# Retention and two gated layers on one core: the causal mask formed on the chip instead of loaded, with fewer warming products and other due times

## The chip, the core and the metric

One core of a Trainium2 chip runs the whole program in one launch. The metric is device time in microseconds (us), the median of three runs; lower is better. Before the change it is 601.28 us (600.91 to 601.75). The engines are named as the profile names them: PE (TensorE, products) with its weight loads PEld, DVE (VectorE), ACT (ScalarE), POOL (GpSimd) and SP (SyncE, which only issues transfers here); SPq, ACTq and POOLq are their transfer queues.

## The reference, cut to what matters

Three steps follow one another on 1536 tokens (2 batches of 768) of width 512, which is 8 heads of 64. The first is a retention layer: a state per head that decays by `gamma[h]` at each step.

```python
gamma = 1.0 - 2.0 ** (-5.0 - np.arange(H))
for t in range(S):
    state = gamma[None, :, None, None] * state + np.einsum('bhd,bhe->bhde', k[:, :, t], v[:, :, t])
    y[:, :, t] = scale * np.einsum('bhd,bhde->bhe', q[:, :, t], state)      # scale = 1/8
x = (x @ w_a) * (x @ w_b) @ w_out                                           # 512 -> 1536 -> 512
xn = x / sqrt(mean(x * x) + 1e-6) * rms_g
out = silu(xn @ w_gate) * (xn @ w_val) @ w_out2                             # 512 -> 1536 -> 512
```

## The kernel before

**Retention in chunks.** The tokens are cut into 12 chunks of 128 (`NCH`, two batches interleaved). For chunk n the kernel forms scores k·q of all heads by eight products of 64 rows (`scores`, banks `sc{n}_0` and `sc{n}_1`), multiplies them on DVE by a mask (`p{n}`), and multiplies the values by that (`values`, `ya{n}`). The mask is, for row s and column t of a chunk, scale·gamma^(t−s) where t is at least s, and 0 elsewhere; it is 128 x 1024 numbers, the same for all chunks. What came before the chunk enters by the running state `st` (`state`, from `vd{n}`, the values decayed by DVE or POOL), copied to `sd`, and by decayed queries `qd` (`past`). One more table, `dq_sb`, is formed on the chip already: `decays` multiplies two small matrices loaded as `tables` and copies the result.

**The two gated layers.** They are blocked by 128 hidden columns and 512 tokens; most blocks use a seven-product scheme in place of eight (names P1 to P7, banks `b`, `d`, `x_P`), the first and last blocks of a layer are plain (`c`, `y`). Weights come as 64-bit words (`raw`), are turned into floats by ACT and DVE (`low`, `top`, `middle`, `joined`), and are split into a high and a low part (`uh`, `ul`), so that each product is done in three passes.

**The order of the work.** Nothing is issued as it is written. Each call goes to `Plan.record` as an operation with a cost; at the end `Plan.order` gives every operation a due time, working back from PE's own order (`dues`), adds the number that the table `SHIFTS` holds for that operation's index, and lists the operations of each engine by readiness and due time (`list`). Adding or removing one operation renumbers all later ones. Each engine then runs its list strictly in order. For the retention part the order of recording is the string `HEAD`: `lq0` loads the queries and keys of chunk 0, `lk0` its keys and values in the other layout, `lw` one weight block, `m` is `masks`, `warm13` is thirteen products of a zero tile (`keep_warm`), `S0` the scores of chunk 0, `d` is `decays`, `L1` both loads of chunk 1, `x` steps the weight conversion.

**The loads at the start.** SP issues the mask (512 KB), then `q0`, `raw0_0`, `q1`, `k0`, `k1` of 512 KB each; ACT issues `dg_sb` (decay factors for values, and others), POOL issues `tables`. PE begins with the warming products, which wait for nothing but a memset of DVE.

Of the kernel before, what the change touches and what calls it, by code (L numbers as in the profile page):

```python
# [10 lines left out]
F32 = mybir.dt.float32  # L11
# [10 lines left out]
B, H, S, D = 2, 8, 768, 64  # L22
P = 128
# [3 lines left out]
C = 128  # L27
NCH = NT // C
CPB = S // C
NP = H // 2  # L30
KD = DM // P
NF = DFF // P
TB = 512
# [6 lines left out]
KH = KD // 2 * P  # L40
# [4 lines left out]
TURN = {(64, P): 200, (64, 64): 110, (P, P): 222, (P, 64): 147}  # L45
TABLE = 1283
SHIFTS = {
# [20 lines left out]
}  # L68
ROUNDS = 2
SLOW = 3414  # L70
# [12 lines left out]
LINE = 128  # L83
# [1 line left out]


FIRST = (0, 0), (0, 1), (1, 0), (1, 1)
HEAD = "lq0 lw m lk0 warm13 S0 d L1 lq3 lq2 lk2 x c0 x x lw lk3 x W0 P0 V0 F0 x w1 S1 Q2 L4 x T0 lw lw P1 V1 F1 T1 x x Ha0 S2 P2 V2 F2 Q3 w2 c0 S3 x T2 W3 P3 x x V3 F3 x S4 x T3 L5 L6 D2 Q4 W4 L7 c1 Ua0 x Q5 W5 T4 x Hb0 Ub0 x D3 G0 S5 P4 V4 R0 F4 x L8 Q6 W6 x S6 T5 P5 V5 F5 c1 x L9 Q7 w7 x T6 S7 P6 V6 F6 x L10 D4 Q8 W8 P7 T7 V7 F7 S8 x x L11 q9 W9 x t0 t1 c1 x x Ua1 Ub1 G1 x x S9 P8 R1 x D5 T8 q10 V8 F8 x t1 c1 Ua2 x x Ub2 x G2 x R2 S10 P9 V9 F9 x q11 t1 T9 x Ua3 x x Ub3 G3 S11 x R3 T10 P10 P11 V10 F10 x x t1 V11 F11"
UP = {"P1": (1, 0), "P2": (5, 1), "P6": (4, 2), "P7": (3, 3), "P5": (2, 4), "P3": (7, 5), "P4": (6, 6)}


# [407 lines left out]


@with_exitstack
def retention_glu_swiglu(ctx: ExitStack, tc: tile.TileContext, qk, kv, tb, mask, dg, eye, w1, w2, rg, partial, out):
    nc = tc.nc
    plan = Plan(nc, tc, ctx)

# [27 lines left out]
    vec, act, gps = Engine("vec", 70, 1.04), Engine("act", 100, 0.83), Engine("gps", 120, 2.2)  # L533

    def dma(engine, out, a, regions=(), **k):
        n = 4
        for size in (out if isinstance(out, View) else a).shape:
            n *= size
        kind = "load" if isinstance(out, View) else "acc" if k else "store"
        plan.record(engine, "dma_start", out, (a,), k, 700 if engine == "gps" else 400, n / RATE[kind], kind, regions)  # L540

    def mm(out, *a, **k):
        n = 1
        for size in out.shape[1:]:
            n *= size
        work["pe"] += 0.443 * n if n >= HB else 111
        full = out.shape[0] == P and a[0].shape[0] == P
        each = 0.443 * n if n > HB else 123.6 if n == HB else 111 if full else 111 * (n + 8) / 136 if out.shape[0] == P or a[0].shape[0] == P else 54
        if n == TB and a[0].tile.dtype == F32:
            each = 0.97 * n  # L550
        if n < HB and full and a[0].tile.dtype == F32:
            each = 232
        op = plan.record("pe", "matmul", out, a, k, each, each + 163)
        op.shape = a[0].shape[0], out.shape[0]
# [11 lines left out]
    one = Pool(plan, "one", 1)  # L566
# [822 lines left out]
    if True:  # L1389

        xf = {}
        if True:
# [3 lines left out]

            dq_sb = ac.tile([P, NP, C], F32, name="dq_sb")
            mask_sb = ac.tile([P, 2, NP, C], F32, name="mask_sb")
            dg_sb = ac.tile([P, 3 * LINE // 4], F32, name="dg_sb")
            tables = one.tile([P, 8, KH], F32, tag="uh1", name="tables").rearrange("p k n -> p (k n)")[:2, :P + TB]  # L1400
            dk_sb = dg_sb[:, :CPB * H].rearrange("p (c h) -> p c h", h=H)
            gq_sb = dg_sb[:, CPB * H:CPB * (H + NP)].rearrange("p (c n) -> p c n", n=NP)
            st = bank("S", "st").rearrange("p (b n d) -> p b n d", b=B, n=NP)
            qk_t, kv_t = {}, {}
# [157 lines left out]
            vec.memset(warm, 0.0)  # L1562
            vec.memset(ones32, 1.0)
            act.activation(both[:, n + KD:n + KD + 2], ones32, AF.Sqrt)
            dma("act", dg_sb[:, :CPB * (H + NP)], dg)
            dma("gps", tables, tb)

            def masks(_):
                dma("sp", mask_sb.rearrange("p r n c -> p (r n c)"), mask)

            def decays(_):
                b = bank("A", "decays")
                plan.cut()
                mm(b, tables[:, :P], tables[:, P:], start=True, stop=True)
                plan.follow(plan.group, firsts[0])
                plan.cut()
                act.copy(dq_sb, b.rearrange("p (n c) -> p n c", n=NP))
# [100 lines left out]
def _consts(np):  # L1678
    g = 1.0 - 2.0 ** (-5.0 - np.arange(H, dtype=np.float64))
    t = np.arange(C, dtype=np.float64)  # L1680
    scale = 1.0 / np.sqrt(D)
    up = scale * g[:, None] ** (C + t - S // 2)
    tb = np.concatenate([np.repeat(np.eye(2), D, axis=1), up.reshape(NP, 2, C).transpose(1, 0, 2).reshape(2, NP * C)], axis=1)
    apart = t[None, :] - t[:, None]
    mask = np.where(apart >= 0, scale * g[:, None, None] ** np.maximum(apart, 0), 0)
    mask = mask.reshape(NP, 2, C, C).transpose(2, 1, 0, 3).reshape(C, 2 * NP * C)
    c = np.arange(CPB)[:, None] * C
    dk = g ** (S // 2 - (c + t)[:, :, None]).transpose(1, 0, 2)
    gq = np.repeat((g ** (c - C)).reshape(CPB, NP, 2, 1), D, axis=3).reshape(CPB, NP, P).transpose(2, 0, 1)
    dg = np.concatenate([dk.reshape(P, CPB * H), gq.reshape(P, CPB * NP)], axis=1)  # L1690
    return {n: np.ascontiguousarray(a, dtype=np.float32) for n, a in (("tb", tb), ("mask", mask), ("dg", dg), ("eye", np.eye(P)))}

# [40 lines left out]
```

## Time and profile before

| | us |
|---|---|
| median of 3 runs (lowest, highest) | 601.28 (600.91, 601.75) |
| the profiled execution | 601.72 |
| its span, first to last instruction | 599.9 |
| PE busy (share of the span) | 593.8 (99%) |
| DVE busy | 526.2 (88%) |
| ACT busy | 427.0 (71%) |
| POOL busy | 118.1 (20%) |

The profile is one execution. Busy time of PE is modelled from starts, so a busy PE need not be a PE at its full pace. The profiled execution took 1.8 us more than its span, and it lies near the slowest of the three timed runs. The chain of work that ended last is PE for 98% of the span.

### The profile page before, as it was taken

How to read it: one execution, taken by the hardware profiler on the slowest of the kernel's cores; microseconds unless marked ns; L12 is line 12 of the kernel's file. 1: busy time of each engine (PE TensorE's matmuls, PEld its weight loads, DVE VectorE, ACT ScalarE, POOL GpSimd, SP SyncE). 2: the span in 40 equal slices, each digit the busy share in tenths (PEclk: the TensorE clock that was granted, in tenths of full speed). 3: DMA queues.
4: the chain of work that ended last, by engine and by line, in shares of the span. 5: the costliest groups of instructions: out<-in, count | busy, mean ns of one | idle time of the engine just before them, and what ended most of it. 6: DMA issues, size and time to landing. Idle time of an engine off the chain costs nothing.

```text
span 599.9 us, 9471 instructions
## 1 busy us (share of the span) xinstructions
PE 593.8 (99%) x3342; PEld 496.0 (83%) x3342; DVE 526.2 (88%) x1012; ACT 427.0 (71%) x822; POOL 118.1 (20%) x135
## 2 busy tenths in 40 slices
PE   9999999999999999999999999999999999999997
PEld 8988888888888888888887888888888888888886
DVE  4898995898999999996799999799999999799874
ACT  5666874668787877867555986768988887786730
POOL 2420000014233323233100000003222232322310
PEclk9999999999999999999999999999999999999999
DMA  8894333148889979799930234317988998985886
GB/s 347 324 348 128 110 109 131 61 105 158 178 153 228 184 140 193 142 168 180 284 136 0 86 127 146 135 70 137 178 154 149 174 184 157 187 157 127 153 198 224
DMA packets 40351, 98.24 MB, mean 164 GB/s; under 512 B 4590, under 2 KB 4974, under 8 KB 40304
## 3 DMA queue, kind: packets, MB, share of 16 engines
q0 software_dynamic: 17312, 31.47, 35.7%
q1 hardware_dynamic: 22704, 66.07, 32.8%
q8 instruction: 26, 0.43, 0.3%
q14 instruction: 21, 0.17, 0.1%
q10 hardware_dynamic: 288, 0.10, 0.1%
HBM read 56.73 MB, written 40.89 MB: 163 GB/s over the span
## 4 chain that ended last, share of the span: by engine, by line
PE 98%; DVE 1%; ACT 0%; issue 0%
PE b L498 32%; PE y L498 18%; PE d L498 16%; PE x_P L498 13%; PE c L498 11%; PE ya L498 3%; PE sc L498 2%; PE w L498 1%; PE st L498 1%; PE ms L498 0%; PE rb L498 0%; DVE acc L498 0%; DVE sq L498 0%; DVE g L498 0%; PE decays L498 0%
## 5 line engine op out<-in xcount | busy, mean ns | idle before, releaser
L498 POOL DMA_DIRECT2D out<-z x60 | 52.2, 894 | 233.2 <-ACT z L498 166.7
L498 POOL DMA_DIRECT2D partial<-z x60 | 52.5, 916 | 202.1 <-ACT z L498 166.3
L498 PE MATMUL y<-h,o 128*128 128x512 f32 (+2 forms) x294 | 70.8, 389 | 0.7 <-DVE h L498 0.7
L498 ACT COPY z<-x_P 128x512 f32<-128x512 f32 x88 | 51.3, 588 | 19.5 <-PE x_P L498 18.4
L498 PEld LDWEIGHTS y<-h,o 128*128 128x128 f32 x294 | 53.6, 188 | 11.9 <-DVE h L498 1.2
L498 DVE TENSOR_TENSOR g<-g,d 128x256 f32<-128x256 f32 x134 | 55.2, 414 | 9.3 <-ACT g L498 6.8
L498 PE MATMUL b<-xh,uh 128*128 128x512 f32 x160 | 63.1, 394 | 0.0
L498 PE MATMUL b<-xh,ul 128*128 128x512 f32 x160 | 62.6, 392 | 0.0
L498 PE MATMUL b<-xl,uh 128*128 128x512 f32 x160 | 62.6, 391 | 0.0
L498 PE MATMUL d<-x,uh 128*128 128x512 f32 (+1 forms) x176 | 59.1, 375 | 0.4 <-DVE g L498 0.4
L498 DVE TENSOR_TENSOR ul<-wt,uh 128x512 fp32r<-128x512 f32 x82 | 54.6, 684 | 2.3 <-ACT uh L498 2.0
L498 ACT CAST v<-raw 128x512 f16<-128x512 bf16 x72 | 55.6, 785 | 0.6
L498 ACT CAST uh<-wt 128x512 fp32r<-128x512 f32 x82 | 49.5, 622 | 5.7 <-DVE wt L498 3.8
L498 ACT ACTIVATE v<-raw 128x512 int32<-128x512 uint32 x72 | 47.9, 680 | 7.8 <-DMA raw<-in_w 7.8
L498 PE MATMUL x_P<-r,l 128*128 128x512 f32 x192 | 52.5, 391 | 0.0
L498 ACT COPY z<-y 128x512 f32<-128x512 f32 x56 | 32.7, 588 | 21.6 <-PE y L498 20.1
L498 PE MATMUL y<-h,l 128*128 128x512 f32 x192 | 47.6, 392 | 0.0
L498 PE MATMUL b<-th,uh 128*128 128x512 f32 x120 | 47.2, 393 | 0.0
L498 PE MATMUL b<-th,ul 128*128 128x512 f32 x120 | 46.9, 391 | 0.0
L498 PE MATMUL b<-tl,uh 128*128 128x512 f32 x120 | 46.8, 390 | 0.0
L498 PE MATMUL d<-x,ul 128*128 128x256 f32 x160 | 44.7, 280 | 0.0
L498 PE MATMUL d<-t,uh 128*128 128x512 f32 (+1 forms) x132 | 44.3, 375 | 0.0
(157 smaller groups left out, 1432.3 us busy)
## 6 DMA issues: line engine op xcount, KB each, us to landing
raw<-in_w SPq DMA_DIRECT2D x72, 512.0 KB, 4.8
partial<-z POOLq DMA_DIRECT2D x60, 256.0 KB, 5.5
out<-z POOLq DMA_DIRECT2D x60, 256.0 KB, 5.4
q<-in_qk SPq DMA_DIRECT2D x12, 512.0 KB, 6.4
k<-in_kv SPq DMA_DIRECT2D x10, 512.0 KB, 7.1
partial<-z SPq DMA_DIRECT2D x12, 256.0 KB, 2.4
acc<-partial SPq DMA_DIRECT2D x6, 512.0 KB, 7.5
out<-z SPq DMA_DIRECT2D x12, 256.0 KB, 2.2
```

Source lines behind the costliest of these rows:

```text
L498: getattr(self.engines[op.engine], method)(real(out), *map(real, args), **{k: real(a) for k, a in kwargs.items()})
```

## The change

The mask's transfer is gone. `tables` grows from 2 x 640 numbers to 8 x 1792 (57,344 bytes for 5,120): gamma^−s per head, the two rows used before, and scale·gamma^t laid out so that an eight-row product of the first with one half of the last gives scale·gamma^(t−s) for four heads at once. Two such products (`mask0`, `mask1`, 128 x 512 each) go to PE ahead of the first scores, and DVE multiplies each by a triangle of ones, `tri`, which travels as 128 more columns of `dg_sb` (114,688 bytes for 36,864). Both transfers are now issued by ACT, `tables` first; POOL issues none at the start. The warming products are 8 instead of 13. The planner's cost for a 512-column product of this kind is 2.05 ns a column instead of 0.97, and `SHIFTS` holds other numbers for other indices.

```diff
-HEAD = "lq0 lw m lk0 warm13 S0 d L1 ...
+HEAD = "lq0 lw lk0 warm8 m S0 d L1 ...
@@ SHIFTS (one row of the table)
-    7: -7450, 8: 9900, 17: 14150, 19: 23600, 22: 17750, 39: 16550, 40: 26600, ...
+    18: -6200, 20: 14750, 22: 21950, 25: 15950, 29: 9950, 42: 14050, 43: 21250, ...
@@ mm
-            each = 0.97 * n
+            each = 2.05 * n
@@
-            dg_sb = ac.tile([P, 3 * LINE // 4], F32, name="dg_sb")
-            tables = one.tile([P, 8, KH], F32, tag="uh1", name="tables").rearrange("p k n -> p (k n)")[:2, :P + TB]
+            dg_sb = ac.tile([P, 3 * LINE // 4 + C], F32, name="dg_sb")
+            tables = one.tile([P, 8, KH], F32, tag="uh1", name="tables").rearrange("p k n -> p (k n)")[:H, :tb.shape[1]]
+            tri = dg_sb[:, 3 * LINE // 4:]
@@
-            dma("act", dg_sb[:, :CPB * (H + NP)], dg)
-            dma("gps", tables, tb)
+            dma("act", tables, tb)
+            dma("act", dg_sb, dg)
             def masks(_):
-                dma("sp", mask_sb.rearrange("p r n c -> p (r n c)"), mask)
+                for r in range(2):
+                    b = bank("Y", f"mask{r}")
+                    plan.cut()
+                    mm(b, tables[:, :P], tables[:, 2 * P + r * TB:2 * P + (r + 1) * TB], start=True, stop=True)
+                    plan.cut()
+                    mult(mask_sb[:, r], b.rearrange("p (n c) -> p n c", n=NP), tri[:, None, :].to_broadcast([P, NP, C]))
@@ decays
-                mm(b, tables[:, :P], tables[:, P:], start=True, stop=True)
+                mm(b, tables[:2, P:2 * P], tables[:2, 2 * P + 2 * TB:], start=True, stop=True)
@@ _consts
+    tb[:, :P] = g[:, None] ** -t
+    for h in range(H):
+        at = 2 * P + (h % 2 * NP + h // 2) * C
+        tb[h, at:at + C] = scale * g[h] ** t
+    tri = t[None, :] >= t[:, None]
```

On SP the mask's issue, the first of its queue, is gone, and `q1` stands ahead of `raw0_0`: `q0`, `q1`, `raw0_0`, `k0`, `k1`.

PE at the start of the program, before (the number behind a name is the chunk, `w` the warming bank; the last number tells tiles apart):

```order
L498 MATMUL w_88<-warm_78 128x128 [waits DVE_49]
L498 MATMUL w_88<-warm_78 128x128 x12
L498 MATMUL sc0_0_115<-q0_102 128x128 [waits DMAHW2_49]
...
L498 MATMUL decays_129<-tables_82 128x512 [waits DMASW0_49]
L498 MATMUL sc1_0_137<-q1_107 128x128 [waits DMAHW4_49]
...
L498 MATMUL ya0_0_157<-p0_131,k0_109 64x128 [waits DMAHW5_49,DVE_49]
...
L498 MATMUL st_174<-vd0_167,k0_109 64x64 [waits DVE_49]
```

The same stretch of PE after the change:

```order
L496 MATMUL w_86<-warm_78 128x128 [waits DVE_49]
L496 MATMUL w_86<-warm_78 128x128 x7
L496 MATMUL mask0_106<-tables_80 128x512 [waits DMAHW0_49]
L496 MATMUL mask1_108<-tables_80 128x512
L496 MATMUL sc0_0_112<-q0_82 128x128 [waits DMAHW1_49]
...
L496 MATMUL decays_129<-tables_80 128x512
L496 MATMUL sc1_0_137<-q1_97 128x128 [waits DMAHW2_49,DVE_49]
...
L496 MATMUL st_156<-vd0_147,k0_102 64x64 [waits DMAHW5_49,DVE_49]
```

Five warming products went and two mask products came, which wait for the table on ACT's queue; the state's update of chunk 0 moved ahead of `ya0`; and the scores of chunk 1 now also wait for DVE, since the mask products took two banks of their ring.

DVE at the start, before (`u0_0` is the first weight block, `vd0` the decayed values of chunk 0):

```order
L498 TENSOR_SCALAR u0_0_125<-raw0_0_105 128x512 [waits DMAHW3_49]
L498 TENSOR_TENSOR p0_131<-sc0_0_115,mask_sb_84 128x512 [waits DMAHW1_49,PE_49]
L498 TENSOR_TENSOR p0_131<-sc0_1_117,mask_sb_84 128x512 [waits PE_49]
L498 ISA u0_0_125<-u0_0_125,v0_0_127 128x1024 [waits DVE_49,Activation_49]
L498 TENSOR_TENSOR p1_153<-sc1_0_137,mask_sb_84 128x512 [waits PE_49]
L498 TENSOR_TENSOR vd0_167<-k0_109,dg_sb_80 128x512 [waits DMAHW5_49,DMAHW0_49]
```

The same stretch of DVE after the change:

```order
L496 TENSOR_TENSOR mask_sb_110<-mask0_106,dg_sb_95 128x512 [waits DMAHW3_49,PE_49]
L496 TENSOR_TENSOR mask_sb_110<-mask1_108,dg_sb_95 128x512 [waits PE_49]
L496 TENSOR_SCALAR u0_0_125<-raw0_0_100 128x512 [waits DMAHW4_49]
L496 TENSOR_TENSOR p0_131<-sc0_0_112,mask_sb_110 128x512 [waits DVE_49,PE_49]
L496 TENSOR_TENSOR p0_131<-sc0_1_114,mask_sb_110 128x512 [waits DVE_49,PE_49]
L496 TENSOR_TENSOR vd0_147<-k0_102,dg_sb_95 128x512 [waits DMAHW5_49]
```

Two multiplications stand ahead of everything else on DVE, and `vd0` moved ahead of the second half of the weight conversion (`ISA`) and of `p1`.

PE where the first output products `y` of layer one begin, before (each `y` is six products, of which the first three are shown):

```order
L498 MATMUL y0_1121<-h0_0_0_475,o0_858 128x512 x3
...
L498 MATMUL b1_0_1136<-xh0_0_170,uh2_1129 128x512
...
L498 MATMUL y3_1149<-h0_0_0_475,o0_858 128x512 x3
...
L498 MATMUL y8_1163<-h0_0_2_1134,o0_858 128x512 x3
...
L498 MATMUL d1_6_1181<-x0_2_784,uh2_1129 128x512
```

The same place of PE after the change:

```order
L496 MATMUL y0_1118<-h0_0_0_471,o0_846 128x512 x3
...
L496 MATMUL y1_1132<-h0_0_0_471,o0_846 128x512 x3
...
L496 MATMUL y3_1146<-h0_0_0_471,o0_846 128x512 x3
...
L496 MATMUL y4_1160<-h0_0_1_751,o0_846 128x512 x3
...
L496 MATMUL y6_1174<-h0_0_1_751,o0_846 128x512 x3
```

Nine of the twelve `y` (0, 1, 3, 4 and 6 to 10) now follow one another before the first `d1_6` and `b1_0`; before, they were spread between those.

## Rows read from the trace of the kernel before

**Rows 1.** The page, part 1: busy us of PE, its weight loads, and others.

```profile
PE 593.8 (99%) x3342; PEld 496.0 (83%) x3342; DVE 526.2 (88%) x1012; ACT 427.0 (71%) x822; POOL 118.1 (20%) x135
```

**Rows 2.** Waits of PE: engine, tile, whom it waited for, us, times, longest.

```profile
PE w L498 <- DVE small L498: 1.1, 1, 1.1
PE y L498 <- DVE h L498: 0.7, 1, 0.7
PE d L498 <- DVE g L498: 0.4, 1, 0.4
PE st L498 <- DVE vd L498: 0.3, 1, 0.3
PE rb L498 <- DVE scale L498: 0.2, 1, 0.2
```

**Rows 3.** Stretches: busy PE, PEld, DVE, ACT, POOL; granted clock, DMA share, GB/s.

```profile
0.00:5.00 5.00, 3.94 (x18) 3.94 (x19) 0.17 (x2) 1.49 (x2) 0.88 (x5) 1.00 0.61 210
5.00:8.00 3.00, 3.00 (x26) 2.78 (x24) 0.43 (x1) 0.78 (x2) 0.00 (x0) 1.00 1.03 421
8.00:12.00 4.00, 3.65 (x46) 2.41 (x46) 3.50 (x6) 3.34 (x9) 0.85 (x1) 1.00 1.03 417
```

**Rows 4.** Timeline, first 12 us, PE: start, us, tile, count, [idle before].

```profile
1.06 5.92 PE L498 MATMUL w<-warm 128*128 128x128 f32 x26 [1.06 <-DVE small L498]
6.90 1.31 PE L498 MATMUL sc<-q 64*128 64x128 f32 x16
8.14 1.12 PE L498 MATMUL decays<-tables 2*128 2x512 f32 x2
9.19 1.16 PE L498 MATMUL sc<-q 64*128 64x128 f32 x16
10.28 1.09 PE L498 MATMUL ya<-p,k 128*64 128x128 f32 x16
11.73 0.69 PE L498 MATMUL st<-vd,k 128*64 128x64 f32 x16 [0.35 <-DVE vd L498]
```

**Rows 5.** Tile w: ns of one, least/median/most.

```profile
L498 PEld LDWEIGHTS w<-warm x26: 288/333/333, 1.1 to 6.3; 128*128 128x128 f32 x26
L498 PE MATMUL w<-warm x26: 421/421/582, 1.1 to 6.6; 128*128 128x128 f32 x26
```

**Rows 6.** The page, part 5: groups, busy us and mean ns of one.

```profile
L498 ACT COPY z<-y 128x512 f32<-128x512 f32 x56 | 32.7, 588 | 21.6 <-PE y L498 20.1
L498 PEld LDWEIGHTS y<-h,o 128*128 128x128 f32 x294 | 53.6, 188 | 11.9 <-DVE h L498 1.2
```

**Rows 7.** Timeline, first 12 us, SPq, ACTq and DVE.

```profile
0.74 0.38 SPq L498 DMA_DIRECT2D mask_sb<-in_mask  x1
0.74 0.41 ACTq L498 DMA_DIRECT2D dg_sb<-in_dg  x1
7.19 0.43 DVE L498 TENSOR_SCALAR u<-raw 128x512 int32<-128x512 int32 x1 [6.18 <-DMA raw<-in_w]
8.24 1.29 DVE L498 TENSOR_TENSOR p<-sc,mask_sb 128x512 f32<-128x512 f32 x2 [0.63 <-PE sc L498]
10.99 0.68 DVE L498 TENSOR_TENSOR vd<-k,dg_sb 128x512 f32<-128x512 f32 x1
```

**Rows 8.** Transfers: issuer, count, KB each, median us from issue to landing.

```profile
mask_sb<-in_mask SPq DMA_DIRECT2D x1, 512.0 KB, 3.9
dg_sb<-in_dg ACTq DMA_DIRECT2D x1, 36.0 KB, 4.0
tables<-in_tb POOLq DMA_DIRECT2D x1, 5.0 KB, 4.8
```

**Rows 9.** Waits of PE's weight loads.

```profile
PEld ya L498 <- issue: 1.6, 7, 0.4
PEld sc L498 <- DMA q<-in_qk: 0.8, 1, 0.8
```

More of the change, by code (lines that the diff above doesn't have):

```diff
@@ L87 @@
 FIRST = (0, 0), (0, 1), (1, 0), (1, 1)
-HEAD = "lq0 lw m lk0 warm13 S0 d L1 lq3 lq2 lk2 x c0 x x lw lk3 x W0 P0 V0 F0 x w1 S1 Q2 L4 x T0 lw lw P1 V1 F1 T1 x x Ha0 S2 P2 V2 F2 Q3 w2 c0 S3 x T2 W3 P3 x x V3 F3 x S4 x T3 L5 L6 D2 Q4 W4 L7 c1 Ua0 x Q5 W5 T4 x Hb0 Ub0 x D3 G0 S5 P4 V4 R0 F4 x L8 Q6 W6 x S6 T5 P5 V5 F5 c1 x L9 Q7 w7 x T6 S7 P6 V6 F6 x L10 D4 Q8 W8 P7 T7 V7 F7 S8 x x L11 q9 W9 x t0 t1 c1 x x Ua1 Ub1 G1 x x S9 P8 R1 x D5 T8 q10 V8 F8 x t1 c1 Ua2 x x Ub2 x G2 x R2 S10 P9 V9 F9 x q11 t1 T9 x Ua3 x x Ub3 G3 S11 x R3 T10 P10 P11 V10 F10 x x t1 V11 F11"
+HEAD = "lq0 lw lk0 warm8 m S0 d L1 lq3 lq2 lk2 x c0 x x lw lk3 x W0 P0 V0 F0 x w1 S1 Q2 L4 x T0 lw lw P1 V1 F1 T1 x x Ha0 S2 P2 V2 F2 Q3 w2 c0 S3 x T2 W3 P3 x x V3 F3 x S4 x T3 L5 L6 D2 Q4 W4 L7 c1 Ua0 x Q5 W5 T4 x Hb0 Ub0 x D3 G0 S5 P4 V4 R0 F4 x L8 Q6 W6 x S6 T5 P5 V5 F5 c1 x L9 Q7 w7 x T6 S7 P6 V6 F6 x L10 D4 Q8 W8 P7 T7 V7 F7 S8 x x L11 q9 W9 x t0 t1 c1 x x Ua1 Ub1 G1 x x S9 P8 R1 x D5 T8 q10 V8 F8 x t1 c1 Ua2 x x Ub2 x G2 x R2 S10 P9 V9 F9 x q11 t1 T9 x Ua3 x x Ub3 G3 S11 x R3 T10 P10 P11 V10 F10 x x t1 V11 F11"
 UP = {"P1": (1, 0), "P2": (5, 1), "P6": (4, 2), "P7": (3, 3), "P5": (2, 4), "P3": (7, 5), "P4": (6, 6)}
@@ L501, in retention_glu_swiglu @@
 @with_exitstack
-def retention_glu_swiglu(ctx: ExitStack, tc: tile.TileContext, qk, kv, tb, mask, dg, eye, w1, w2, rg, partial, out):
+def retention_glu_swiglu(ctx: ExitStack, tc: tile.TileContext, qk, kv, tb, dg, eye, w1, w2, rg, partial, out):
     nc = tc.nc
@@ L1682, in _consts @@
     up = scale * g[:, None] ** (C + t - S // 2)
[L1683 to L1686, printed above, removed]
+    tb = np.zeros((H, 2 * P + 3 * TB))
+    tb[:, :P] = g[:, None] ** -t
+    tb[:2, P:2 * P] = np.repeat(np.eye(2), D, axis=1)
+    for h in range(H):
+        at = 2 * P + (h % 2 * NP + h // 2) * C
+        tb[h, at:at + C] = scale * g[h] ** t
+    tb[:2, 2 * P + 2 * TB:] = up.reshape(NP, 2, C).transpose(1, 0, 2).reshape(2, NP * C)
+    tri = t[None, :] >= t[:, None]
     c = np.arange(CPB)[:, None] * C
@@ L1689, in _consts @@
     gq = np.repeat((g ** (c - C)).reshape(CPB, NP, 2, 1), D, axis=3).reshape(CPB, NP, P).transpose(2, 0, 1)
-    dg = np.concatenate([dk.reshape(P, CPB * H), gq.reshape(P, CPB * NP)], axis=1)
-    return {n: np.ascontiguousarray(a, dtype=np.float32) for n, a in (("tb", tb), ("mask", mask), ("dg", dg), ("eye", np.eye(P)))}
+    dg = np.concatenate([dk.reshape(P, CPB * H), gq.reshape(P, CPB * NP), np.zeros((P, 3 * LINE // 4 - CPB * (H + NP))), tri], axis=1)
+    return {n: np.ascontiguousarray(a, dtype=np.float32) for n, a in (("tb", tb), ("dg", dg), ("eye", np.eye(P)))}
 def _layout(np, i):
```

38 rows, old and new, of the table SHIFTS are left out of this document.

## The prediction

> **What bounds the kernel now.** I read the page's busy times first: PE is busy for 593.8 of 599.9 us [rows 1], so a change pays only if it takes work from PE or one of the few times that PE waits. The list of PE's waits comes next, and it is short [rows 2]: 1.1 us at the very start, 0.3 for the decayed values of chunk 0, and 0.7, 0.4 and 0.2 (1.3 together) between the two layers. No transfer stands in it. One looks as if it did: the weight loads of the scores waited 0.8 for a query load [rows 9]; but in that time PE itself was working at `decays`, from 8.14 to 9.19 [rows 4], and that is the weight loader's wait alone. The loads are nevertheless at their limit there: the DMA share is 1.03 and 417 to 421 GB/s between 5 and 12 us [rows 3]. So at the start PE and the loads run level, PE a little behind.
>
> Then the first 12 us of PE's timeline [rows 4]: 13 warming products from 1.06 to 6.90 (26 records, 0.449 us a product), scores of chunk 0 for 1.24 to the next start, `decays` 1.05, scores of chunk 1 for 1.09, and on to `ya0` at 10.28. The pace changes in it. [...] The first scores took 0.15 longer than the second, so the rise fell inside them: 0.15 lost at half pace is 0.3 us, which puts it at about 7.2 in this execution.
>
> **The change part by part.** The sum is made on the profiled execution, 601.72 us for a span of 599.9; it is 0.44 above the median of 601.28.
>
> Five warming products go: 5 x 0.449 = 2.25 us off PE's path, and PE comes to the masks at 1.06 + 8 x 0.449 = 4.65.
>
> Two mask products come. `decays` is the nearest row, 512 columns of two rows: 1.05 us at the upper level [rows 4]. The lower bound for the pair is 2.10; the upper, all of it at half pace, 4.20. If the rise stays at 7.2, 2.55 us at half pace do 1.28 of the 2.10 and the other 0.82 follows at full pace: 3.37, so the first scores start at 8.02 and not 6.90, +1.12. They then run at full pace, −0.15. I take that eight rows cost what two do; if time went by rows, the pair would be four times 2.10, and the forecast would be far off. [...]
>
> The wait for chunk 0's decayed values, 0.35 [rows 4], should go: `k0` comes earlier, `vd0` stands earlier on DVE. −0.35, and at least 0. What could be late in its place is DVE: the mask multiplications are 0.65 each (two in 1.29 [rows 7]), the second ends near 8.02 + 0.65 = 8.7, the weight step (0.43) at 9.1, just when the scores of chunk 0 end (8.02 + 1.09 = 9.11); then `p0` 1.29, to 10.4, and `vd0` 0.68, to 11.1. PE ends the scores of chunk 1 at 9.11 + 1.05 + 1.09 = 11.25. So the state's update finds `vd0` done, with 0.15 to spare; were it not, all of PE's list stands behind it, and the cost is what `vd0` is late. The new wait of chunk 1's scores for DVE (the ring's banks) asks for the multiplications by 10.16, which leaves 1.4. The weight step on DVE moves from 7.19 to about 8.7; `c0_0_0`, which needs it in the end, now has the scores of chunk 2 ahead of it.
>
> That move of the scores of chunk 2 costs two more changes of product shape. The nearest row is the weight loader's issue wait at such changes, 1.6 us in 7 [rows 9], 0.23 each; between 0 and 0.46, I take 0.2.
>
> Loads. 524,288 bytes go and 57,344 − 5,120 + 114,688 − 36,864 = 130,048 come; at 417 GB/s that is 1.26 − 0.31 = 0.95 us earlier for every later load of the first stretch. PE waited for none of them, so this buys the 0.35 above and no more. The issues moved to ACT (0.41 each) and off SP and POOL lie where these engines have nothing to do: DVE waits until `raw` lands at 7.19 [rows 7], and ACT's first work is on the same block. The table must be there at 4.65. `dg_sb`, issued in the same place of the same queue, landed 4.0 after its issue at 0.74, at 4.74 [rows 7, 8]; that is the row I go by, and it means a wait of 0.1 at most. By `tables` as POOL loaded it (4.8) it is 5.54; the mask's own 3.9 gives 4.64. The triangle, one issue later and with more bytes, is needed at about 6.8 and has two us to spare by the same row.
>
> Everything behind (new shifts, other orders in the layers) removes and adds no instruction. PE's work there is the same, so I count 0, with bounds: −1.3 if all the waits between the layers went (on DVE the order through that place, from the mean of squares to the scaled rows, reads almost the same as before, which speaks against it) and +1.3 if as many new ones came.
>
> Sum with the rise at 7.2: +1.12 − 0.15 − 0.35 + 0.2 = +0.82. With the rise already at 4.65, before the masks: they cost 2.10, and the five warming products would have cost the old kernel 5 x 0.449 x 188/333 = 1.27, so it would come to its scores at 5.92 and the new one at 6.75. But the old one would then meet its loads: the mask landed at 4.64, and at 1.26 each `q0`, `raw0_0`, `q1` and `k0` come at 5.9, 7.2, 8.4 and 9.7 (an estimate from [rows 3, 8]). Its `ya0` would start at 9.7, and the wait for `vd0` remains; the new kernel ends the scores of chunk 1 at 6.75 + 1.09 + 1.05 + 1.09 = 9.98. 9.98 − 9.7 − 0.35 + 0.2 = +0.1. The profiled execution is near the slowest of its three runs, so the median is likely one with an earlier rise; I take the middle of the two, +0.45, on the median: 601.28 + 0.45 = 601.7 us.
>
> [...]
>
> **The rivals.**
>
> An exact exchange: the masks do the warming's duty, the transfer was hidden, and the early loads return what half pace takes. For it: the lower bound of the masks, 2.10, is about the 2.25 removed. Against: the half-pace part above. Down to 2.10 − 2.25 − 0.35 = −0.5, so 600.8 to 601.3.
>
> The table late, the rise put off (slower). PE has nothing between the eighth warming product and the table. It decides from a landing after 4.65. If it lands as POOL's did, at 5.54, PE idles 0.89; with the rise still at 7.2 the masks end at 5.54 + 1.66 + 1.27 = 8.47, +1.57 − 0.15 − 0.35 + 0.2 = +1.3, or 602.6. If the idle stretch puts the rise off behind the masks, they take 4.20 and end at 9.74: +2.84 − 0.35 + 0.2 = +2.7, or 604.0. For it: an eight-row transfer on this queue is not in the trace, and one of 5 KB took 4.8 us. Against: the queue's own row, 4.0. [...]
>
> New waits in the layers (slower). Nine `y` now stand together ahead of the products that need the second weight pair, and the fillers are spent sooner. For it: DVE is 88% busy, so a late conversion has little to catch up with. Against: each `y` needs one copy of 588 ns on ACT [rows 6], which is 71% busy. At +1.3 on the forecast, 603.0.
>
> The waits between the layers go (faster): 601.28 − 1.3 − 0.5 = 599.5.
>
> **How the numbers follow.** Forecast 601.7, 0.41, its own range 601.3 to 602.2; exact exchange 0.23; table late 0.14, half of it at each price; new waits 0.12; waits gone 0.10. A measurement of this kernel can tell about 0.2% from no change, 1.2 us: below 600.1 is faster, above 602.5 slower. Faster is the last case, 0.10; slower is 0.14 + 0.10 of the two slower rivals, 0.24; the rest, 0.66, is the same. For the range I leave out the waits-gone case below (0.10) and the 604.0 half of the late table with a little of the new waits above (0.09): 600.4 to 603.2.
>
> **What would show it.** In the changed profile: warming products end near 4.65 and the first mask product follows within 0.1; the two masks take between 2.1 and 3.4 us, and the first scores start between 6.8 and 8.1; PE waits nowhere for `vd`; its busy time is within 1 us of 593.8 and the waits between the layers are still about 1.3. An idle PE ahead of the masks would show the table late. First scores at or before 6.5, or `mask` products under 1 us each, would prove the price wrong, and PE waits of a us or more after 20 us would prove the 0 for the layers wrong.

## The result: slower, and outside the forecast range

The changed kernel takes 605.27 us (median of 6 runs, 603.48 to 606.47) against 601.17 (6 runs, 600.85 to 601.75) for the kernel before: a ratio of 1.0059, 95% interval 1.0047 to 1.0072. The forecast was 601.7 with a range up to 603.2. The profiled execution after took 605.89 us for a span of 604.1; the six runs spread over 3 us, and the rows below are of this one.

The busy times come first, in the form of [rows 1].

```profile
PE 598.5 (99%) x3336; PEld 497.8 (82%) x3336; DVE 529.3 (88%) x1014; ACT 425.1 (70%) x822; POOL 117.9 (20%) x134
```

PE is busy for 4.7 us more, though it has three products fewer. The waits of PE answer [rows 2]:

```profile
PE w L496 <- DVE small L496: 1.1, 1, 1.1
PE y L496 <- DVE h L496: 0.7, 1, 0.7
PE d L496 <- DVE g L496: 0.4, 1, 0.4
PE rb L496 <- DVE scale L496: 0.2, 1, 0.2
```

No wait is new, those between the layers are the same three, and the 0.3 for `vd` is gone. So the loss is not in a wait: the same work took longer. Where, the start of PE's timeline shows, in the form of [rows 4].

```profile
1.06 3.78 PE L496 MATMUL w<-warm 128*128 128x128 f32 x16 [1.06 <-DVE small L496]
4.77 3.78 PE L496 MATMUL mask<-tables 8*128 8x512 f32 x4
8.48 2.08 PE L496 MATMUL sc<-q 64*128 64x128 f32 x16
10.48 2.07 PE L496 MATMUL decays<-tables 2*128 2x512 f32 x2
12.48 2.08 PE L496 MATMUL sc<-q 64*128 64x128 f32 x16
14.49 1.12 PE L496 MATMUL st<-vd,k 128*64 128x64 f32 x16
15.40 2.41 PE L496 MATMUL ya<-p,k 128*64 128x128 f32 x32
17.64 0.63 PE L496 MATMUL st<-vd,k 128*64 128x64 f32 x16
18.20 1.16 PE L496 MATMUL sc<-q 64*128 64x128 f32 x16
...
22.02 1.10 PE L496 MATMUL ya<-qd,sd 64*64 64x128 f32 x32
```

Read the durations of equal shapes down this list. Sixteen products of the scores take 2.08 at 8.48 and at 12.48, and 1.16 at 18.20; `decays` takes 2.07, where it took 1.12 [rows 4]; the second states take 0.63, the first 1.12. PE worked at half pace, as the state with scores of 2.08 is called here, until some point within `ya` (15.40 to 17.64), where before it was at full pace (scores of 1.16) from the middle of the first scores. There is no idle mark from the warming products on. The stretches, in the short form for PE alone (busy us, granted clock, DMA share, GB/s), say the same of its time:

```profile
0.00:5.00 5.00, 3.94 (x17) 1.00 0.64 196
5.00:8.00 3.00, 3.00 (x4) 1.00 1.03 402
8.00:12.00 4.00, 4.00 (x19) 1.00 0.79 294
12.00:18.00 6.00, 6.00 (x79) 1.00 0.96 356
```

From 5 to 18 us PE is busy for 13.00 of 13 us. The granted clock reads 1.00 in all four, as it did before [rows 3], while the scores take 2.08 for 1.16. The two do not contradict each other: the trace's own list for the clock has its first entry, at level 1.0, only at 16.41 us (7.24 before), its one other entry, at level 0.5, is at 603.50, and the stretches read 1.00 where there is no entry. The durations change at just these times, so I read the half pace as level 0.5 and the first entry as the clock's rise, 9.2 us later than before.

How much of the loss lies here? The first product with `qd` is the first mark behind the changed start. It stood here in the kernel before:

```profile
17.29 1.10 PE L498 MATMUL ya<-qd,sd 64*64 64x128 f32 x32
```

22.02 − 17.29 = +4.73. From there to the end of the span it is 604.1 − 22.0 = 582.1 after and 599.9 − 17.3 = 582.6 before, −0.5. All of the loss of this execution, and a little more, is in the first 22 us.

### The profile page after: what moved, and what is told of

The parts are those of the page before. It is cut to its first block, busy times and chain, and to the rows that moved or that the text cites. A ratio compares the mean times of both kernels' runs of the same rounds, so it can differ in the third digit from the quotient of the medians.

```text
span 604.1 us, 9462 instructions
## 1 busy us (share of the span) xinstructions
PE 598.5 (99%) x3336; PEld 497.8 (82%) x3336; DVE 529.3 (88%) x1014; ACT 425.1 (70%) x822; POOL 117.9 (20%) x134
## 4 chain that ended last, share of the span: by engine, by line
PE 98%; DVE 1%; ACT 0%; issue 0%
PE b L496 32%; PE y L496 18%; PE d L496 16%; PE x_P L496 13%; PE c L496 11%; PE ya L496 3%; PE sc L496 2%; PE st L496 1%; PE w L496 1%; PE mask L496 1%; PE ms L496 0%; PE decays L496 0%; PE rb L496 0%; DVE acc L496 0%; DVE sq L496 0%; DVE g L496 0%
```

## Experiments

Nine kernels ran, each in five rounds beside the kernel before; their diffs are shortened here. Theory A: PE does not come up to full pace on the products of few rows that took the place of five warming products. Rival B: the rest of the change (loads, orders, shifts) costs the time.

**The masks with all 13 warming products.**

```diff
-                for _ in range(n):                       # n = 8
+                for _ in range(13):                      # the order is still planned for 8
                     mm(w, warm, warm, start=True, stop=True)
```

> The changed kernel with 13 warming products again ahead of the two mask products; the order on every engine is kept as in the changed kernel. Theory A (the clock stayed at the lower level because the eight warming products were followed by products of few rows, not by more full ones): the warming ends near 6.9, the upper level comes at about 7.2 as before, the masks then take about 2.1 us, first scores at about 9.0, and the time is 602.3 (601.6 to 603). Rival B (the rise was put off by something else in the change, as the earlier loads or the other order): the first 16 us stay at half pace and the five products cost 2.2 more: 606 to 608.

Measured: 603.02 us (602.88 to 604.0), ratio 1.0029 [1.0018, 1.0040]. The start of PE's timeline:

```profile
1.06 5.24 PE L496 MATMUL w<-warm 128*128 128x128 f32 x26 [1.06 <-DVE small L496]
6.23 1.98 PE L496 MATMUL mask<-tables 8*128 8x512 f32 x4
8.14 1.16 PE L496 MATMUL sc<-q 64*128 64x128 f32 x16
9.23 1.12 PE L496 MATMUL decays<-tables 2*128 2x512 f32 x2
```

```profile
PE st L496 <- DVE vd L496: 0.6, 1, 0.6
PE ya L496 <- ACT uh L496: 0.5, 1, 0.5
```

Five products added to the changed kernel made it some 2 us faster. The scores and `decays` behind the warming run at full pace, 1.16 and 1.12 (the clock's first entry stands at 5.44, within the warming), and the pair of masks takes 8.14 − 6.23 = 1.91 us there. The time is just above A's range (603): the two waits above, 0.6 and 0.5, were not in the estimate. B's 606 to 608 did not come, though the rest of the change is in this kernel too; the 1.5 us that are left over the kernel before are not taken apart here.

**Eight warming products in the kernel before, the mask still loaded.** 

```diff
-                for _ in range(n):                       # n = 13
+                for _ in range(8):                       # the order is still planned for 13
                     mm(w, warm, warm, start=True, stop=True)
```

> The kernel before with 8 warming products instead of 13, the mask still loaded, order kept as before. Theory A in the form that the full products were too few: PE idles from 4.65 to the landing of the first queries (about 5.9), the rise comes well after 7.2, scores of chunk 0, decays and scores of chunk 1 take about 2 us each, and the time is 603 to 604.5. Theory A in the form that only the mask products are to blame, and rival B: the rise stays near 7.2 and the time is 600.6 to 601.3, since the first scores start a little earlier.

Measured: 603.67 us, ratio 1.0027 [1.0013, 1.0042]; its 12 runs lie from 600.89 to 605.39. The profiled one is at half pace through `decays` (2.07) and both scores (2.08 each):

```profile
1.06 3.78 PE L498 MATMUL w<-warm 128*128 128x128 f32 x16 [1.06 <-DVE small L498]
5.74 2.08 PE L498 MATMUL sc<-q 64*128 64x128 f32 x16 [0.90 <-DMA q<-in_qk]
7.75 2.07 PE L498 MATMUL decays<-tables 2*128 2x512 f32 x2
```

The time is in A's first range, and the clock's first entry is at 13.34. So the five products mattered without any mask, though not in every run: five of the twelve took 602.04 us or less. And PE also stood idle for 0.90 here, so this kernel alone does not tell an idle engine from products of few rows.

**Thirteen warming products of 8 rows in the kernel before.** Nothing else differs, and PE has as much to do for as long.

```diff
-                    mm(w, warm, warm, start=True, stop=True)
+                    mm(w, warm[:8], warm[:8], start=True, stop=True)   # recorded with the shape and times of 128 rows
```

> The kernel before with its 13 warming products on 8 rows of the tile instead of 128, as many, as long and in the same order; nothing else differs. Theory A (few-row products do not bring the clock up): the first scores still start near 6.9, but PE stays at half pace far behind 7.2, and the time is 603.5 to 606. Rival C (any busy PE brings it up): 601.2, with the rise at about 7.2.

Measured: 606.61 us (605.83 to 607.12), ratio 1.0084 [1.0072, 1.0096]: above A's range (606), and far from rival C's 601.2.

```profile
1.06 5.91 PE L498 MATMUL w<-warm 8*128 8x128 f32 x26 [1.06 <-DVE small L498]
6.90 2.08 PE L498 MATMUL sc<-q 64*128 64x128 f32 x16
8.91 2.07 PE L498 MATMUL decays<-tables 2*128 2x512 f32 x2
10.91 2.08 PE L498 MATMUL sc<-q 64*128 64x128 f32 x16
12.91 1.89 PE L498 MATMUL ya<-p,k 128*64 128x128 f32 x16
```

The products take 5.91 us as before (5.92 [rows 4]), the scores start at the same 6.90, and from there on all runs at half pace into `ya`; the clock's first entry is at 14.59. This is a loss like that of the changed kernel, and larger, made in the old one by the rows alone, with no idle stretch, no mask and no other load. PE was busy from 1.06 to 12.91 without a gap and still at half pace: in this execution 11.85 us of busy time alone did not bring the clock up.

**The changed kernel with masks of 128 rows.** The table is loaded as 32 rows (eight of them used), zeros stand in the other 96, and the two mask products read all 128. Eight warming products, as in the change.

```diff
+            # zeros in tables[32:64] by VectorE, in tables[64:] by GpSimd
-                    mm(b, tables[:8, :P], tables[:8, 2 * P + r * TB:2 * P + (r + 1) * TB], ...)
+                    mm(b, tables[:, :P], tables[:, 2 * P + r * TB:2 * P + (r + 1) * TB], ...)
```

> The changed kernel with its two mask products taken over all 128 rows, 120 of them zero (the table is loaded as 32 rows, the others are cleared on DVE and POOL), same results, same number of products, order kept. 172 KB more are loaded, which PE should not feel. Theory A: the upper level comes near 7.2, the masks take about 3.4 us together, first scores near 8.0, and the time is 601.2 to 602, which is what was forecast for the change. Rival B or C: as the changed kernel, 605.3.

Measured: 602.01 us (601.55 to 603.93), ratio 1.0017 [1.0007, 1.0027].

```profile
1.06 3.39 PE L496 MATMUL w<-warm 128*128 128x128 f32 x16 [1.06 <-DVE warm L496]
4.93 1.96 PE L496 MATMUL mask<-tables 128*128 128x512 f32 x4 [0.47 <-DMA tables<-in_tb]
6.82 1.16 PE L496 MATMUL sc<-q 64*128 64x128 f32 x16
7.91 1.12 PE L496 MATMUL decays<-tables 2*128 2x512 f32 x2
8.96 1.16 PE L496 MATMUL sc<-q 64*128 64x128 f32 x16
11.05 0.69 PE L496 MATMUL st<-vd,k 128*64 128x64 f32 x16 [0.93 <-DVE vd L496]
```

Rows of zeros gave back 2.5 us by the ratios, 3.3 by the medians. The pair takes 6.82 − 4.93 = 1.89 us, as long as with 8 rows at full pace. A's time is met within 0.01, but not its way (a rise near 7.2, masks of 3.4): in this execution the clock rose at 3.90, within the warming, whose products span both paces.

```profile
L496 PE MATMUL w<-warm x16: 274/421/583, 1.1 to 4.2; 128*128 128x128 f32 x16
```

So this trace shows neither that masks of 128 rows bring the clock up nor that an idle 0.47 ahead of them does no harm. That their rows mattered is shown by the times: 18 of the 23 runs of this kernel and of the next, which has the same products, took under 603 us, and none of the six of the changed kernel did. The larger table and the clearing, which also differ, were not tried without the rows.

The runs show more. Four of the twelve took 603.52 to 603.93 us, and their mean granted clock is 0.997; the other eight, 601.55 to 602.47, have 0.999 or 1.000. The missing 0.003 of 602 us, at level 0.5, is an estimated 3.6 us on record at that level, which would cost 1.8. Three of the six runs of the changed kernel have 0.994, an estimated 7 us. When in those runs this lay is not on record. The 16.41 us ahead of the first entry did not count in the mean of the changed kernel's profiled execution: it is 0.999, and at level 0.5 they alone would make it an estimated 0.986. So a clock that rose and fell again in those runs is my reading; the trace of that execution has its one fall at 603.50, near its end.

When the clock rose, by the first entry of each trace, and what PE was on:

| kernel | us | PE at that time |
|---|---|---|
| before | 7.24 | first scores |
| the change | 16.41 | `ya` |
| 13 warming products and masks | 5.44 | warming |
| 8 warming products, mask loaded | 13.34 | `ya` |
| 13 warming products of 8 rows | 14.59 | `ya` |
| masks of 128 rows | 3.90 | warming |
| the same, early triangle | 5.09 | masks |

In the three late cases the rise came 1.92, 1.58 and 1.68 us after the start of the first products of 128 rows behind the scores (`st` in the change, `ya` in the other two).

**Is what is left the triangle?** In that run VectorE waits long for the load that brings the decays and the triangle:

```profile
7.58 1.29 DVE L496 TENSOR_TENSOR mask_sb<-mask,dg_sb 128x512 f32<-128x512 f32 x2 [5.00 <-DMA dg_sb<-in_dg]
```

So this load went first on SyncE's queue, and `u` behind `vd` on VectorE:

```diff
-            dma("act", dg_sb, dg)        # second on ScalarE's queue
+            dma("sp", dg_sb, dg)         # first on SyncE's queue
...
-  VectorE: mask, mask, u, p, p, vd
+  VectorE: mask, mask, p, p, vd, u
```

> The changed kernel with mask products of 128 rows (as in the run before, 602.01 us), and with two moves in the head: the load of the decays and the triangle goes first on SyncE's queue in place of second on ScalarE's, and VectorE converts the first weights (u) after the first two of its products with the mask and the decayed values (vd), not before them. VectorE waited 5.00 us for that load and TensorE 0.93 us for vd. Theory A (that load alone holds up the head): the wait at the first states goes or falls under 0.2, the second states end 0.6 to 0.9 us earlier, and the time is 601.0 to 601.5, level with the kernel before or a little under it. Rival E (VectorE has too much to do there, and the wait only moves to the second past products or to the converted weights): 601.8 to 602.3, no change.

Measured: 602.03 us (601.42 to 604.07), ratio 1.0014 [1.0004, 1.0023]. The wait for `vd` fell from 0.93 to 0.31 and a wait of 0.26 came at the second `ya`; no gain in the median. Rival E's number holds, though the wait itself did fall. The two traces are not alike ahead of it: the clock rose at 3.90 there and at 5.09 here.

**The loads alone.** The kernel before without its mask load:

```diff
-  dma("sp", mask_sb, mask)
+  GpSimd writes a constant into mask_sb, in the same place of the order
```

> The kernel before (13 warming products) without the load of the mask: a constant is written into the mask's tile by GpSimd instead, so the mask's values are left out of the result; every other instruction stays in its place on each engine, and what SyncE loads behind the mask starts one load earlier. Theory A (the earlier loads are worth the wait of 0.35 us at the first states and nothing else, since TensorE reaches each later load with its data there): 600.8 to 601.5, at most 0.4 us below the kernel before. Rival D (the loads of the head bound more than that wait, and part of what the changed kernel gains behind the head comes from them): 600.4 or less.

Measured: 602.4 us (600.36 to 603.58), ratio 1.0013 [1.0002, 1.0024]. Rival D falls; A is missed too, since the time rises. Its waits:

```profile
PE b L502 <- DVE v L502: 0.6, 1, 0.6
PE st L502 <- DVE vd L502: 0.6, 2, 0.4
PE c L502 <- DVE ul L502: 0.5, 1, 0.5
```

The first states still wait, and two waits further on are new. Why loads one place earlier bring these was not looked into. They bring no gain.

**The price of the masks taken away.** The table in bf16 (each power as three pieces, 48 rows of pairs), so that each mask and the decays are one bf16 product; 11 warming products, and in a second kernel 13.

```diff
-  tables: 32 rows of f32, loaded; mask and decays products in f32; 8 warming products
+  tables: 64 rows of bf16, loaded (zeros below); the products in bf16; 11 (13) warming products
```

> The run before (128-row masks, early triangle, 602.03 us) with a table in bf16: each power of g is the sum of three bf16 pieces, six pairs of pieces stand in 48 rows, and each mask and the decays are one bf16 product in place of an f32 one; 11 warming products in place of 8. TensorE took 1.98 us for the two f32 masks and 1.05 us for the decays at full pace; consecutive 256-column products of the c tiles start 0.12 us apart, so 512 columns should take 0.24 us and the three products 0.7 us in place of 3.0. Theory A (what the masks cost the changed kernel is their products on TensorE ahead of the first scores, and the half pace at which they ran): the first scores start at 6.9 us at the latest, the decays are 0.8 us shorter, the st wait doesn't come back by more than half of it, and the time is 600.4 to 601.1, under the kernel before. Rival E (VectorE, with two more products in the head, holds up the states and the second past products whatever TensorE does): 601.3 to 602.0.

> The same kernel with 13 warming products. Theory A: the clock is up before the masks or during them, the scores start 0.3 to 0.5 us later than with 11 and the time is 600.7 to 601.4; if the executions of the kernel with 11 spread up to 602 or above and these don't, the spread is that of the clock's rise. Rival E: 601.3 to 602.0, as with 11.

Measured: 601.60 us (601.5 to 603.51), ratio 1.0010 [1.0001, 1.0018], and with 13, 601.68 (601.14 to 603.6), ratio 1.0009 [1.0000, 1.0018]. With 11:

```profile
5.91 0.59 PE L504 MATMUL mask<-tables 128*128 128x512 bf16 x2
6.43 1.16 PE L504 MATMUL sc<-q 64*128 64x128 f32 x16
7.53 0.39 PE L504 MATMUL decays<-tables 32*128 32x512 bf16 x1
7.84 1.16 PE L504 MATMUL sc<-q 64*128 64x128 f32 x16
10.68 0.69 PE L504 MATMUL st<-vd,k 128*64 128x64 f32 x16 [1.68 <-DVE vd L504]
```

The masks take 0.52, the decays 0.31, the scores are through 1.3 us earlier than before, and the gain ends in a wait of 1.68. What VectorE waited for then:

```profile
9.94 0.69 DVE L504 TENSOR_TENSOR vd<-k,dg_sb 128x512 f32<-128x512 f32 x1 [1.02 <-DMA k<-in_kv]
```

a load. Theory A's time is missed. Rival E named the place rightly, but not the reason: VectorE was idle. Both kernels have runs above 603.5, so two more warming products don't take that spread away. With 11 it goes with the clock: the three runs above 602 have a mean granted clock of 0.997, the other eight 0.999 or 1.000. With 13 the longest (603.6) has 0.997 too, but 602.45 and 602.83 have 1.000; what made those longer stays open.

**That load moved ahead.** 

```diff
-  SyncE: dg, q0, q1, raw0_0, k0, k1      VectorE: p, p, vd, u, u+v, p, p
+  SyncE: dg, q0, k0, q1, raw0_0, k1      VectorE: p, p, vd, p, p, u, u+v
   ScalarE: the weights' v behind the decays' copies, uh behind the first xh
```

> The run with bf16 masks and 11 warming products (601.60 us), where TensorE stood 1.68 us before the first states for vd, and VectorE 1.02 us before vd for the first load of k. Moved here: SyncE loads k0 ahead of q1 in place of behind q1 and the first weights; ScalarE converts the weights (v) after the decays' copies and uh after the first xh; VectorE multiplies the second scores (p) ahead of the weights' u, and takes ul after the first xl. Theory A (since TensorE is no longer the limit of the head, the order in which its 512 KB loads land is): the st wait falls to 0.6 us or less, the first qd product starts 0.6 to 1.1 us earlier (at 16.8 to 17.3 us by the profile), and the time is 600.5 to 601.1, under the kernel before. Rival F (what k0 gains, the second k or the weights lose, and the wait moves to the second past products or the c tiles): 601.4 to 602.

Measured: 601.84 us (601.26 to 602.56), ratio 1.0004 [0.9995, 1.0013]. The wait for `vd` is gone, and two others are there:

```profile
8.88 1.16 PE L518 MATMUL sc<-q 64*128 64x128 f32 x16 [0.74 <-DMA q<-in_qk]
...
13.92 1.16 PE L518 MATMUL sc<-q 64*128 64x128 f32 x16 [0.61 <-DMA q<-in_qk]
```

Rival F's time holds; its place does not, since PE waits for queries, at the scores. With masks of 0.52 (11 warming products) and 0.74 (here) PE came before a 512 KB load had done its part in both orders tried: 1.68 for `vd`, which waited 1.02 for `k`, then 0.74 and 0.61 for `q`. None of the nine beats the kernel before; the last can't be told from it.

## Why the prediction was wrong

**The step that failed: "If the rise stays at 7.2, 2.55 us at half pace do 1.28 of the 2.10 and the other 0.82 follows at full pace", and "They then run at full pace, −0.15".** I took the rise as a moment that busy PE reaches, so that eight-row masks would serve as well as the warming they replace. For the kernel before, 7.2 was read rightly (7.24). That the pace ahead of the rise is half of that behind it, on which the 7.2 and the 1.28 rest, was my estimate, and no row before shows it; the runs showed scores of 2.08 and 1.16 and the levels 1.0 and 0.5. They also showed that these masks did not serve: the clock rose at 16.41, and PE stayed at half pace through the masks and on into `ya`. By the starts, the masks took 8.48 − 4.77 = 3.71 (3.37 forecast); scores, `decays` and scores took 14.49 − 8.48 = 6.01 where I had 3.23; states and `ya` lost the rest. The scores of chunk 1 end at 14.49, not at my 11.25, 3.24 us later; the profiled execution missed the sum made on it, 601.72 + 0.82, by 3.35.

**The lower case of the range.** The sum with an early rise (+0.1) had the same fault: both ends assumed that the rise would come no later than before. It scales the warming by two weight loads, 188 ns [rows 6] and 333 [rows 5]. That the median run has an earlier rise than the profiled one, which put the forecast midway, no run shows, since one execution of the kernel before has its rise on record (7.24); the two kernels with masks of 128 rows, with the same products, rose at 3.90 and 5.09. A late rise stood only in the rival "table late", and hung there on an idle PE. That an idle stretch puts the rise off no row before shows; the one run with both (0.90 idle, rise at 13.34) does not tell it from products of few rows. That rival named the right direction, and came nearest with its price (604.0), by a cause that did not occur: the masks start at 4.77 with no wait. That is luck: it priced half pace for the masks alone, and scores and `decays` at half pace stood in no term.

**The masks' size was right.** The forecast was 2.10 for the pair at full pace, from `decays`; it measured 1.91 with 8 rows and 1.89 with 128. That eight rows cost what two do was taken with no row before to show it; in these runs eight cost what 128 did. What went with the rows of the warming was the pace behind it: scores of 2.08 behind 8 rows, 1.31 and 1.16 [rows 4] behind 128.

**Five warming products, 2.25 us.** They were priced as time that PE would get back. The kernel with 8 of them and the loaded mask (1.0027) shows that they were not free to take: PE first waited 0.90 for `q`, then ran at half pace (scores of 2.08).

**The 0.35 at the states went,** but the reason given fails in part: it was 0.35 again with the mask's load gone, so earlier loads alone did not remove it. In the changed kernel PE came to the states at 14.49, long after `vd` (11.79 + 0.68 = 12.47).

**The triangle "has two us to spare": wrong,** with no cost in this kernel. I went by the landing of 4.0 us [rows 8]. The row after and the work behind it:

```profile
dg_sb<-in_dg ACTq DMA_DIRECT2D x1, 112.0 KB, 6.3
7.77 1.50 DVE L496 TENSOR_TENSOR mask_sb<-mask,dg_sb 128x512 f32<-128x512 f32 x2 [6.76 <-DMA dg_sb<-in_dg]
```

VectorE began the mask multiplications at 7.77, not at 6.8. The scores at half pace covered it; with full pace, in the run of 128-row masks, PE waited 0.93 for `vd`, of which 0.31 was left once the triangle came early and `u` stood behind `vd`.

**The layers at 0: right.** Behind the first `qd` product it is −0.5 us, with the same three waits of 1.3 together; neither the new waits nor their loss came. The +0.2 for changes of product shape shows in no row by itself.

## What to carry over

The filler products ahead of this kernel's first work had an effect beyond their own time. Before trading them for useful work of another shape, compare durations of one shape behind them, not the busy share, and look for the first entry of the clock; here 13 products of 8 rows filled the same time as 13 of 128 (5.91 and 5.92 us), the clock rose 7.69 us behind the start of the scores (6.90 to 14.59), and the ratio was 1.0084. And price a removed product by what is late next: when the masks took 0.52 on PE, a wait of 1.68 behind the load of k, and with k ahead waits of 0.74 and 0.61 for q, took back the whole gain.

## What was not expected of the hardware

- PE, busy without a gap for 5.84 us on products of 8 rows, and on scores, `decays` and `ya` behind them, was at half pace until 14.59; behind the same products on 128 rows the clock rose at 7.24 (scores of 1.31 and 1.16 [rows 4], 2.08 each behind 8 rows). Zeros were enough in these runs: the warming tile holds nothing else, and the clock rose on it at 3.90 with the masks of 128 rows and at 5.44 with 13 warming products and masks.
- The granted clock of the changed kernel's stretches from 0 to 18 us reads 1.00 while the scores in them take 2.08 for the later 1.16; the trace has no entry for the clock ahead of 16.41. Two durations of one shape showed the pace here, and the first entry showed when it changed.
- A load of 112 KB took 6.3 us to land as the second on ScalarE's queue while 512 KB loads ran, and 4.1 as the first on SyncE's, in the kernel with the early triangle (2.3 in that with bf16 masks and 11 warming products).
